# One nine-slot ring for K, V and all weights, K^T written in place, and P·V with V as the stationary operand

## The chip, the cores and the metric

One NeuronCore of a Trainium2 chip. The metric is the device time of one execution in microseconds (us). The engines are written as the profile writes them: PE is TensorE (PEld its weight loads), DVE VectorE, ACT ScalarE, POOL GpSimd, SP SyncE, which here issues the loads; PSUM is the memory that PE writes its results to. Each experiment ran beside the kernel before on the same chip. Ratios are the mean time of one kernel's fast runs over the mean of the other's in the same rounds, so they are not quite the ratios of the medians that I quote. A profile's span is some 2 us shorter than the measured time of the same execution (before: 434.1 against 435.88).

## The reference, cut to what matters

A decode step: one query token, 32 query heads over 4 KV heads, 65,536 cached positions of 128 dimensions, and beside it a gated MLP on the same x.

```python
q = (x @ wq).reshape(1, 1, 32, 128)             # x: 1x1024, wq: 1024x4096
scores = einsum('bhqd,bhkd->bhqk', q, k) * 128 ** -0.5   # k: 4 x 65536 x 128, each for 8 heads
o = einsum('bhqk,bhkd->bhqd', softmax(scores), v)
a = o.reshape(1, 1, 4096) @ wo
z = gelu(x @ w_in);  b = (z1 * (w_sp * layernorm(z2) + b_sp)) @ w_out
out = g * a + (1 - g) * b                       # g = sigmoid(sum(x * gate_w))
```

All of it is bf16. 162.0 MB are read once: K and V 134.2, wq and wo 8.4 each, w_in 7.3, w_out 3.7. There is one query, so every loaded byte is used once.

## The kernel before

K and V come in chunks of 2.1 MB (8192 positions of one KV head), in the order K0 K1 V0 K2 V1 K3 V2 V3, eight chunks each. A chunk of K is turned by TensorE in groups of eight 128x128 tiles. DVE or ACT evicts a turned group from one of three PSUM banks into a small ring, and the scores are taken from there two groups later.

```python
CFG = dict(NSLOT=5, CHUNK_ROWS=8192, RING=5, TBANKS=3, LAG=2, EVPAT="DDA", NALLD=3)
KV  = A("kvarena", [128, NSLOT, CR], BF16)      # five slots for K and V
RNG = A("ktring", [128, R, GPB * 128], BF16)    # K^T, five groups
W   = A("warena", [128, NW, 8192], BF16)        # four slots for the weights
...
# load of a K or V chunk (SyncE, in order): waits until PE has begun the chunk after the one to be replaced
W_.wait("pe_cons", pos - NSLOT + 1)
eng.dma_start(dst, src).then_inc(sb(it["dmasem"]), 16)
...
# one group of K: eight transposes, then the scores of the group two back
eng.matmul(tb[:, j*128:(j+1)*128], kvv[:, t, :], ident_bf[:, :], start=True, stop=True, is_transpose=True)   # L531
eng.tensor_copy(RNG[:, G % R, :], tb[:, :])             # L585, two of three groups (ACT: L587)
eng.matmul(bank[:, t*REP:(t+1)*REP], RNG[:, G % R, j*128:(j+1)*128], qT_bf[...], start=True, stop=True)      # L550
# per chunk: row maximum and copy of the 128x512 scores (DVE)
eng.tensor_reduce(cmax[:, n, :], bank..., AX.X, ALU.max); eng.tensor_copy(scT[:, n, :], bank[:, :])
...
# P.V: p is stationary (8 columns), V moves (128 columns)                                                       L617
eng.matmul(PO[0:REP, 0:DH], pv[:, t, :], vv[:, t, :], start=(c == 0 and t == 0), stop=(...))
# afterwards o (8x128) is scaled, split into hi and lo (two bf16 parts that add up to it), turned by two matmuls, and multiplied by all of wo
```

Exp runs on ACT over a whole KV head at a time: exp of head g while K or V of others are worked on. V(g) waits for it.

## Time and profile before

| | before |
|---|---|
| time, median | 438.09 us (435.88 to 440.12, 4 runs); 438.47 in 16 runs |
| span of the profiled run | 434.1 us |
| busy PE / DVE / ACT | 341 / 190 / 141 us |
| loads | 162.0 MB, 373 GB/s over the span, 425 GB/s at the plateau |
| last load landed | about 412 to 415 us, then 20 us of PE and DVE work |

No engine is busy all the time. The one thing that is nearly always busy is the stream of loads, and the lines that show this are in the prediction. A line of the slices gives 40 equal parts of the span; a line of the windows gives, for 4 us, the busy time and count of each engine, the clock that the throttle granted to TensorE (1.00 is full), the mean share of the 16 DMA engines, and GB/s.

### The profile page before, as it was taken

What the parts mean: (1) busy time and instruction counts of PE and PEld (TensorE: products, weight loads), DVE (VectorE), ACT (ScalarE), POOL (GpSimd) and SP (SyncE); (2) the same over time, 40 slices, a digit from 0 to 9 for tenths busy, and PEclk for the clock granted to TensorE, in tenths of its full rate; (3) what the DMA queues carried; (4) which work ended last, traced back from release to release, by engine and by line L of the source; (5) the groups of instructions that cost most, each with busy time, mean ns of one, the idle gap of its engine ahead of it and who ended that gap; (6) DMA issues with size and microseconds to landing.
All of it is one profiled execution on the core that took longest, in us unless ns stands there. A gap on an engine that the chain in (4) does not pass through costs nothing.

```text
span 434.1 us, 14443 instructions
## 1 busy us (share of the span) xinstructions
PE 341.1 (79%) x6810; PEld 324.6 (75%) x6810; DVE 190.4 (44%) x357; ACT 141.0 (32%) x131; POOL 0.9 (0%) x8
## 2 busy tenths in 40 slices
PE   0059767879888697989798869668889877999994
PEld 0059666868888597988768769568888777988892
DVE  1006644878978600029848730005988720001304
ACT  1003312429944296010124469200034379000000
POOL 0000000000000000000000000000000000000000
PEclk9999988998999889969899979899999989899999
DMA  7998999999999699989999999999999999999900
GB/s 271 427 430 340 426 421 429 427 423 429 417 341 350 226 355 429 430 325 367 415 360 350 402 404 405 416 430 426 426 424 424 421 346 408 425 430 420 408 12 0
DMA packets 17474, 162.94 MB, mean 375 GB/s; under 512 B 1285, under 2 KB 1285, under 8 KB 8198
## 3 DMA queue, kind: packets, MB, share of 16 engines
q1 hardware_dynamic: 17414, 162.02, 91.5%
q8 instruction: 53, 0.87, 0.8%
q14 instruction: 7, 0.06, 0.0%
HBM read 162.01 MB, written 0.00 MB: 373 GB/s over the span
## 4 chain that ended last, share of the span: by engine, by line
PE 46%; DMA 18%; ACT 18%; DVE 15%; issue 2%; SPq 1%; DVEq 0%; ACTq 0%
ACT scT L720 17%; PE ps_tb L531 16%; PE ps_o L617 14%; DMA kvarena<-in_A_k_cache_dram 13%; PE ps_sc L550 8%; DMA warena<-in_A_wq_dram 5%; DVE ktring L585 4%; DVE cmax L637 4%; DVE scT L639 3%; PE ps_m L970 3%; PE ps_m L490 2%; PE ps_m L789 1%; PE ps_m L887 1%; ACT ktring L587 1%; DVE a_sb L986 0%
## 5 line engine op out<-in xcount | busy, mean ns | idle before, releaser
L531 PE MATMUL ps_tb<-ident_bf,kvarena 128*128 128x128 bf16 x2048 | 160.8, 224 | 11.3 <-DMA kvarena<-in_A_k_cache_dram 10.6
L585 DVE COPY ktring<-ps_tb 128x1024 bf16<-128x1024 bf16 x195 | 126.4, 686 | 35.5 <-PE ps_tb L531 35.3
L617 PE MATMUL ps_o<-kvarena,scT 128*8 128x128 bf16 x2048 | 129.0, 230 | 5.9 <-DMA kvarena<-in_A_v_cache_dram 5.4
L617 PEld LDWEIGHTS ps_o<-kvarena,scT 128*8 128x8 bf16 x2048 | 126.6, 92 | 6.7 <-DMA kvarena<-in_A_v_cache_dram 6.0
L531 PEld LDWEIGHTS ps_tb<-ident_bf,kvarena 128*128 128x128 bf16 x2048 | 121.3, 99 | 12.7 <-DMA kvarena<-in_A_k_cache_dram 11.2
L587 ACT ACTIVATE ktring<-ps_tb 128x1024 bf16<-128x1024 bf16 x61 | 62.7, 1028 | 172.5 <-PE ps_tb L531 172.5
L550 PE MATMUL ps_sc<-qT_bf,ktring 128*128 128x8 bf16 x2048 | 89.1, 167 | 22.1 <-DVE ktring L585 20.5
L550 PEld LDWEIGHTS ps_sc<-qT_bf,ktring 128*128 128x128 bf16 x2048 | 76.7, 97 | 27.9 <-DVE ktring L585 25.7
L720 ACT ACTIVATE scT<-scT,nbias 128x512 bf16<-128x512 bf16 x32 | 74.3, 2737 | 14.5 <-DVE nbias L708 14.5
L637 DVE TENSOR_REDUCE cmax<-ps_sc 128x8 f32<-128x512 f32 x32 | 22.1, 691 | 14.0 <-PE ps_sc L550 11.6
L727 DVE CAST rs_hi<-rowsum 128x8 bf16<-128x8 f32 x4 | 0.7, 170 | 55.8 <-ACT scT L720 55.8
L490 PE MATMUL ps_m<-xgT_bf,warena 128*128 128x1 bf16 x256 | 7.1, 165 | 22.1 <-DMA warena<-in_A_wq_dram 20.5
L760 DVE TENSOR_SCALAR o_sb<-ps_o,rcp 8x128 f32<-8x128 f32 x4 | 1.4, 338 | 52.5 <-PE ps_o L617 52.5
L490 PEld LDWEIGHTS ps_m<-xgT_bf,warena 128*128 128x128 bf16 x256 | 7.0, 104 | 22.3 <-issue 22.3
L639 DVE CAST scT<-ps_sc 128x512 bf16<-128x512 f32 x32 | 21.8, 681 | 0.0
L720 ACT ACTIVATION_READ_ACCUMULATOR scT<-scT,nbias 128x1 f32 x32 | 15.9, 497 | 0.0
L970 PE MATMUL ps_m<-warena,oT_bf 128*1 128x256 bf16 x128 | 12.9, 272 | 1.0 <-DVE oT_bf L953 1.0
L498 DVE CAST qT_bf<-ps_m 128x32 bf16<-128x32 f32 x1 | 0.2, 192 | 28.6 <-PE ps_m L490 28.6
L970 PEld LDWEIGHTS ps_m<-warena,oT_bf 128*1 128x1 bf16 x128 | 9.1, 83 | 3.9 <-DVE oT_bf L953 1.4
L986 DVE TENSOR_TENSOR a_sb<-a_sb,ps_m 1x512 f32<-1x512 f32 x6 | 4.1, 685 | 10.0 <-PE ps_m L970 9.9
L798 DVE COPY zT<-ps_m 128x28 f32<-128x28 f32 x1 | 0.2, 188 | 17.7 <-PE ps_m L789 17.7
L738 PE MATMUL ps_m<-ident_bf,rs_hi 128*8 128x128 bf16 x4 | 0.9, 219 | 8.6 <-DVE rs_lo L730 8.6
(86 smaller groups left out, 52.3 us busy)
## 6 DMA issues: line engine op xcount, KB each, us to landing
kvarena<-in_A_k_cache_dram SPq DMA_DIRECT2D x32, 2048.0 KB, 19.0
kvarena<-in_A_v_cache_dram SPq DMA_DIRECT2D x32, 2048.0 KB, 11.9
warena<-in_A_wq_dram SPq DMA_DIRECT2D x4, 2048.0 KB, 14.4
warena<-in_A_wo_dram SPq DMA_DIRECT2D x4, 2048.0 KB, 18.7
warena<-in_B_w_in_dram SPq DMA_DIRECT2D x4, 1792.0 KB, 19.9
warena<-in_B_w_out_dram SPq DMA_DIRECT2D x2, 1792.0 KB, 16.4
xg_raw<-in_A_x_dram SPq DMA_DIRECT2D x1, 2.0 KB
gw_raw<-in_gate_w_dram SPq DMA_DIRECT2D x1, 2.0 KB
```

The source lines that it names most:

```text
L490: mm_ = eng.matmul(PM0[:, QC + h:QC + h + 1], wv[:, t % 2, h * 128:(h + 1) * 128], xgT_bf[:, t:t + 1], start=(t == 0), stop=(t == KT - 1))
L531: mm_ = eng.matmul(tb[:, j * 128:(j + 1) * 128], kvv[:, t, :], ident_bf[:, :], start=True, stop=True, is_transpose=True)
L550: mm_ = eng.matmul(bank[:, t * REP:(t + 1) * REP], RNG[:, G % R, j * 128:(j + 1) * 128], qT_bf[:, g * REP:(g + 1) * REP], start=True, stop ...
L585: eng.tensor_copy(dst, tb[:, :]).then_inc(sb("ev_dve"), 1)
L587: eng.activation(dst, tb[:, :], ACT.Copy).then_inc(sb("ev_act"), 1)
L617: mm_ = eng.matmul(PO[0:REP, 0:DH], pv[:, t, :], vv[:, t, :], start=(c == 0 and t == 0), stop=(c == CPG - 1 and t == T - 1))
L637: eng.tensor_reduce(cmax[:, n, :], bank[:, :].rearrange("p (t h) -> p h t", h=REP), AX.X, ALU.max)
L639: eng.tensor_copy(scT[:, n, :], bank[:, :]).then_inc(sb("dve_evac"), 1)
L720: eng.activation(ap_in, ap_in, ACT.Exp, bias=nbias[:, gh:gh + 1], scale=SCALE, accum_out=rowsum[:, gh:gh + 1]).then_inc(sb("act_exp"), 1)
L789: mm_ = eng.matmul(PM0[:, ZPC + ft:ZPC + ft + 1], wv[:, t % 2, ft * 128:(ft + 1) * 128], xgT_bf[:, t:t + 1], start=(t == 0), stop=(t == KT ...
L887: mm_ = eng.matmul(PM1[row:row + 1, 0:512], hT_bf[:, u:u + 1], wv[:, u % 7, q * 512:(q + 1) * 512], start=(u == 0), stop=(u == NFH - 1), t ...
L970: mm_ = eng.matmul(PM1[row:row + 1, c0:c0 + 256], oT_bf[:, gh:gh + 1], wv[:, gh % 8, q * 256:(q + 1) * 256], start=(k == 0), stop=(k == RE ...
```

## The change

Intent: no buffer of its own for any kind of data. One ring of nine slots takes K, V and every weight in the order of use, so that the loads run further ahead of PE. K^T is written back over K in the same slot, which replaces the K^T ring. P·V is turned round, so that V is the stationary operand and eight columns of p move; o then comes out as 128x8 and needs no transposition. Weights are used one slot at a time, with partial sums added on DVE. The diff, cut to its core (the large part that only moves code and adds partial sums is left out, lines are shortened, and the comments are mine):

```diff
-    NSLOT=5,  RING=5,  LAG=2,  NALLD=3,
+    NSLOT=9,  NALLD=5,  RS_OFF=6.5,  MAXT_OFF=0.40,  Z_OFF=6,
-    RNG = A("ktring", [128, R, GPB * 128], BF16)
-    W = A("warena", [128, NW, 8192], BF16)
...
+    seq_list = [("W", "wq", i_) for i_ in range(4)] + list(raw)     # raw: K0 K1 V0 K2 V1 K3 V2 V3
+    # w_in goes between the chunks of V0, w_out between those of K2, wo 0..2 into K2, K3 and V3, wo 3 at the end
...
-            if pos - NSLOT + 1 >= 1:
-                W_.wait("pe_cons", pos - NSLOT + 1)
+            if pos >= NSLOT:
+                occ = SEQ[pos - NSLOT]          # K: its scores are done; V and W: its last matmul is done
+                W_.wait(occ["rel"][0], occ["rel"][1])
...
-            dst = RNG[:, G % R, :]
+            dst = KV[:, it["slot"], b * GPB * 128:(b + 1) * GPB * 128]
...  # all eight groups of a chunk are turned first, then the scores of the chunk before
-                    mm_ = eng.matmul(PO[0:REP, 0:DH], pv[:, t, :], vv[:, t, :],
+                    mm_ = eng.matmul(PO[:, g * REP:(g + 1) * REP], vv[:, t, :], pv[:, t, :],
...
-            eng.tensor_scalar(o_sb[0:8, g*DH:(g+1)*DH], PO[0:REP, 0:DH], rcp8[0:8, g:g+1], None, op0=ALU.mult)
+            eng.tensor_tensor(oT_bf[:, g*REP:(g+1)*REP], PO[:, g*REP:(g+1)*REP], rcpb[:, g*REP:(g+1)*REP], ALU.mult)
```

## The prediction

> **What bounds the kernel now.** I read the page's forty slices first, then the time windows of 4 us, then the chain of work that ended last, then the timeline of single stretches, and last the waits of the DMA queue.
>
> The slices:
>
> ```profile
> PE   0059767879888697989798869668889877999994
> DVE  1006644878978600029848730005988720001304
> DMA  7998999999999699989999999999999999999900
> GB/s 271 427 430 340 426 421 429 427 423 429 417 341 350 226 355 429 430 325 367 415 360 350 402 404 405 416 430 426 426 424 424 421 346 408 425 430 420 408 12 0
> HBM read 162.01 MB, written 0.00 MB: 373 GB/s over the span
> ```
>
> A slice is 10.85 us. The load stream runs at a plateau of some 425 GB/s, has holes (slices 4, 12 to 15, 18 to 22, 33), and is over two slices before the kernel is. So the kernel is bound by its one stream of 162.01 MB, plus what that stream loses. At 425.5 GB/s the bytes take 380.7 us. The transfer records of the trace show that rows of 2 KB (w_out, wo; 12 MB) move at some 385 GB/s, which adds 2 us: 383 us. By 8 us the stream has moved 1.72 MB, so it starts, in effect, at 4.0. Hence the span: 4.0 start + 383 stream + 25 holes + 22 tail = 434.
>
> The windows show one hole and the tail (columns: window, busy time of PE, PEld, DVE, ACT, POOL, granted clock, DMA share, GB/s):
>
> ```profile
> 144.00:148.00 4.00, 3.11 (x78) 2.88 (x75) 2.63 (x5) 1.02 (x1) 0.00 (x0) 1.00 0.76 317
> 148.00:152.00 4.00, 1.90 (x17) 1.71 (x18) 1.98 (x8) 1.21 (x1) 0.00 (x0) 0.59 0.24 57
> ...
> 408.00:412.00 4.00, 4.00 (x67) 3.60 (x65) 1.37 (x2) 0.00 (x0) 0.00 (x0) 1.00 0.94 393
> 412.00:416.00 4.00, 4.00 (x75) 4.00 (x73) 0.00 (x0) 0.00 (x0) 0.00 (x0) 1.00 0.11 45
> 416.00:420.00 4.00, 4.00 (x76) 4.00 (x73) 0.00 (x0) 0.00 (x0) 0.00 (x0) 1.00 0.00 0
> 420.00:424.00 4.00, 4.00 (x76) 4.00 (x73) 0.00 (x0) 0.00 (x0) 0.00 (x0) 1.00 0.02 4
> ```
>
> After 412 everything has landed and PE works off a backlog of V chunks at 76 matmuls per 4 us, 53 ns each, 3.4 us per chunk of 64. Adding the shortfall of each window against 425: 2.0 us lost at 32 to 36 (the queue waits in order for w_in behind q), 10.9 at 120 to 160, 3.6 at 188 to 204, 4.1 at 224 to 244, 1.2 at 260 to 276, 2.6 at 348 to 364: about 25.
>
> The chain shows why holes come during K: one K chunk is one row maximum (cmax), and these are 6.2 us apart, while 2.097 MB arrive in 4.93 us.
>
> ```profile
> 304.39 0.69 DVE cmax L637
> ...
> 310.61 0.69 DVE cmax L637
> ...
> 316.82 0.69 DVE cmax L637
> ```
>
> PE lags 1.3 us per K chunk. Five slots fill, and the queue waits:
>
> ```profile
> SPq L512 <- PE ps_tb L531: 186.8, 31, 11.2
> SPq L512 <- PE ps_o L617: 141.8, 27, 10.8
> ```
>
> These sums are mostly harmless (a full ring waits for each slot while four other loads run); only where GB/s falls do they cost.
>
> **What the Trainium skill says.** "DMA: Bandwidth & Descriptors", section Where 436 GB/s comes from, gives 435.2 GB/s as the ceiling of the 16 ports; the trace agrees, its full windows being 422 to 430. "TensorE: Matmul & The Clock Gate", section Weight-path perf modes, says that 128 bf16 weight columns load by the fast path; section Back-to-back issue gap says that pairs of weight load and matmul sustain some 81 ns at N=128. The trace is faster: 53 ns for a V matmul, and 27 ns for a 128x128 weight load with one moving column (q projection, below). Section The HAM clock gate says an idle window halves the clock; the trace agrees (0.59 in the window at 148, after PE idled).
>
> ```profile
> 24.79 5.93 PE ps_m L490 x217
> ```
>
> **The change, part by part.**
>
> *PV turned round.* V becomes the stationary 128x128 operand and eight columns of p move. Today: 64 x 53 = 3.4 us. Afterwards it has the shape of the score matmuls, of which eight start within 0.20 us in the timeline (25 ns each), and of the q projection (5.93/217 = 27 ns): 64 x 27 = 1.75 us per chunk. PE saves 1.65 us on each of 32 chunks, 53 us of work. It is off the path where PE waits for V data, but it lets PE recover 4.93 - 1.75 = 3.2 us of lag per V chunk instead of 1.5, and it removes the backlog at the end. The transposition of o also goes (four times o_hi, o_lo, two matmuls and a copy), some 1.2 us of it in the tail.
>
> *K^T in place, nine slots for everything.* The K^T ring and the four weight buffers become four more slots. A K slot is now held until its scores are done, one chunk later.
>
> *Transposes first, scores of the previous chunk afterwards.* PE's work per K chunk: 64 transposes at 56 ns = 3.6, 64 scores at 26 ns = 1.65: 5.25 us. I walked through one chunk by hand. Maximum and cast take DVE 1.3 us after the scores; PE fills the three banks meanwhile (1.35 us); then each transposed group waits for an eviction. With DVE alone (0.61 us per eviction, 8 in 4.88 us in the timeline) the last group is out at 5.0 and the scores at 6.65 us; with every third eviction on ACT I get 5.8 to 6.3, mean 6.1. So a K chunk takes as long as before (6.2); this part gains nothing itself.
>
> *Does the ring hold the lag?* Worst are the 16 K chunks in a row at the start: five of them by DVE alone (5 x 1.7) and eleven mixed (11 x 1.2) give 8.5 + 13 = 21.5 us, 4.4 chunks. When PE starts chunk n, slots up to n-2 are free, so loads up to n+7 are issued: the stream runs dry only when it is 7 chunks, 34 us, ahead. Next the eight V0 chunks: PE catches up in about 12 us, then stands in front of the sum of exp(1) (16 rows of 18.5 us of ACT plus the maximum chain, less those 12: about 10 us, two chunks). Later K runs start with no lag, gain 10 us by themselves and some 6 from the gelu and layernorm chain, and have 34. So I expect no hole that is worth more than 1 to 3 us.
>
> *Weights in the stream.* In the order of use, as ordinary slots; the partial sums of q, z and b add small vector instructions (0.19 us each for q and z, 0.68 for b), beside other work. The 2 us hole at 32 goes.
>
> *The tail.* Last in the stream is wo3, 2 MB after the last V chunk. V7 is done 1.75 us after it lands, long before wo3. After wo3: 32 matmuls of 256 columns, 3.2 us at full clock (timeline: x32 in 3.22) or some 6.8 at half (PE is busy only 35% by then; 256 columns at half of the 2.4 GHz that the same TensorE page gives is 213 ns each, an estimate), then unchanged 5.2 us from the first a_sb addition at 428.9 to the end at 434.1. Tail: 0.3 + 5 + 5.2 = 10.5 instead of 22.
>
> Sum: 4.0 + 383 + 2 + 10.5 = 399.5 of span; holes -23, tail -11.5. The profiled run was 1.8 us above its span and the median 4 above it: 3 more. But 383 contains my 2 us for narrow rows, some of which the plateau already holds, so I take 401 for the time.
>
> **Rivals.**
> 1. *The ring still fills in the first sixteen K chunks.* If a K chunk takes 7.5 us (a slower clock, DVE and ACT out of step), the lag is 16 x 2.6 = 41 us against 34: 7 us of hole, 409. For it: PE, DVE and ACT are chained by three banks. Against: 6.2 is measured with a deeper coupling.
> 2. *V as weights is slow.* The profile's page gives 97 ns mean for a weight load of 128x128; were it not hidden, V would take 6.2 us a chunk, above the 4.93 of its load: 32 x 1.3 = 41 us, and the gain is gone (about 440). Against: the same shape runs at 25 to 27 ns in two places.
> 3. *Head of line.* All loads now wait in one order, weights too; PE standing in front of exp or the layernorm chain could hold a slot that everything waits for: 5 to 10 us, 406 to 411. The windows at 148 and 188 speak for such standing, nine slots against its reaching the stream.
> 4. *Transfer hidden anyway?* No: the stream is the path, its holes cost one for one.
>
> **Range and chances.** Below: stream at 427 and a warm tail, 394. Above: rival 1 or 3 in part, 411. Only rival 2 leads out of "faster" (429.3 is 2%), and two measured rows speak against it: faster 0.95, same 0.04, slower 0.01.
>
> **What would show it.** Right: GB/s above 415 in nearly all slices from the second on, the last byte at 386 to 392, about 10 us of tail, V matmuls 64 within 2 us with PE idle in front of each, cmax still 6 us apart. Wrong: a slice under 380 around 110 to 150 (rival 1 or 3), V chunks above 4.9 us (rival 2), or a plateau below 420 throughout, which no term of mine holds.

## The result, and the profile after

405.4 us median (404.22 to 406.69, 11 runs) against 438.47 (16 runs): ratio 0.9252, 95% interval 0.923 to 0.9275. Predicted: 401.0, range 394 to 411. Faster, inside the range, and 4 us above the forecast.

The slices of the page after, one slice being 10.1 us:

```profile
PE   0339988978897753778999865499989764336334
PEclk9999999999999655569999975579999855558556
DMA  6999999999999999999999999999999999999940
GB/s 259 427 435 429 429 429 429 425 427 430 427 427 422 371 423 426 421 398 430 411 431 430 429 429 427 427 416 430 429 424 432 427 430 425 420 422 429 422 190 0
```

The holes of before have gone, but for slice 14 (371) and slice 18 (398). Slice 14 is under 380, which the prediction had named as a sign of being wrong (its rivals 1 and 3); in size it is 1.2 us of loads. PE is now idle in the V stretches, where it was busiest before. One thing was not in the forecast: the last slice with traffic runs at half rate. The windows show it (same columns as in the prediction):

```profile
136.00:140.00 4.00, 3.01 (x103) 2.74 (x99) 2.96 (x8) 0.00 (x0) 0.00 (x0) 0.50 0.91 333
140.00:144.00 4.00, 3.81 (x136) 3.70 (x136) 0.17 (x1) 3.65 (x3) 0.00 (x0) 0.50 1.04 419
...
380.00:384.00 4.00, 0.94 (x35) 0.94 (x35) 0.00 (x0) 0.00 (x0) 0.00 (x0) 0.50 1.03 415
384.00:388.00 4.00, 1.05 (x40) 0.96 (x37) 0.00 (x0) 0.00 (x0) 0.00 (x0) 0.50 0.60 243
388.00:392.00 4.00, 1.76 (x64) 1.67 (x63) 0.17 (x1) 0.00 (x0) 0.00 (x0) 0.50 0.48 186
```

From 384 on the DMA share is 0.60 and then 0.48: about half of the 16 engines have nothing left, and the others work on for 8 us. The chain of work that ended last (start, us, what):

```profile
94.75 0.69 DVE cmax L628
...
101.33 0.69 DVE cmax L628
...
120.44 0.69 DVE cmax L628
...
126.81 0.69 DVE cmax L628
...
357.54 35.42 DMA kvarena<-in_A_wo_dram
393.09 5.48 PE ps_m L1017 x31
398.59 0.68 DVE a_sb L1033
```

K chunks are 6.58 us apart where DVE evicts alone, and 6.37 here where ACT takes a third (in the stretch from 42.8 to 80.1 six of them take 37.3 us, 6.2 each). So K is no faster than before. The end is the last load, then 5.48 us for the 32 matmuls of wo 3, one of whose records is missing (before: 3.22), then unchanged vector work.

The timeline of PE (start, us, line, operation, count, and the wait before it) shows V chunks late and early in the kernel:

```profile
378.14 1.87 PE L610 MATMUL ps_o<-scT,kvarena 128*128 128x8 bf16 x64 [3.02 <-DMA kvarena<-in_A_v_cache_dram]
...
140.05 3.76 PE L610 MATMUL ps_o<-scT,kvarena 128*128 128x8 bf16 x135
146.27 3.39 PE L610 MATMUL ps_o<-scT,kvarena 128*128 128x8 bf16 x121 [2.46 <-issue]
```

Late in the kernel a V chunk costs 1.87 us and then waits 3 us for the next load. Early, where PE has a backlog to work off, it runs 135 matmuls, stands 2.46 us for something the profile calls issue, and runs 121 more. The list of waits has this at 21.3 us in V alone:

```profile
PEld ps_o L610 <- issue: 21.3, 9, 3.0
```

### The profile page after: what moved, and what is told of

It is laid out like the page before. It is cut to its first block, busy times and chain, and to the rows that moved or that the text cites.

```text
span 403.8 us, 14317 instructions
## 1 busy us (share of the span) xinstructions
PE 284.9 (71%) x6810; PEld 256.9 (64%) x6810; DVE 186.9 (46%) x368; ACT 152.1 (38%) x142; POOL 0.9 (0%) x8
## 4 chain that ended last, share of the span: by engine, by line
PE 44%; DMA 23%; ACT 15%; DVE 12%; issue 4%; SPq 1%; DVEq 0%
PE ps_tb L528 22%; PE ps_sc L546 13%; ACT scT L775 9%; DMA kvarena<-in_A_wo_dram 9%; DMA kvarena<-in_A_v_cache_dram 8%; DMA kvarena<-in_A_k_cache_dram 6%; ACT kvarena L562 6%; DVE kvarena L560 4%; PE ps_m L1017 3%; PE ps_o L610 3%; DVE cmax L628 3%; DVE scT L630 2%; PE ps_m L865 1%; PE ps_m L981 1%; SPq L510 1%
## 5 line engine op out<-in xcount | busy, mean ns | idle before, releaser
L528 PE MATMUL ps_tb<-ident_bf,kvarena 128*128 128x128 bf16 x2048 | 141.1, 225 | 21.8 <-DVE kvarena L560 10.5
L560 DVE COPY kvarena<-ps_tb 128x1024 bf16<-128x1024 bf16 x184 | 118.5, 685 | 20.3 <-PE ps_tb L528 18.2
L562 ACT ACTIVATE kvarena<-ps_tb 128x1024 bf16<-128x1024 bf16 x72 | 73.6, 1023 | 132.4 <-PE ps_tb L528 132.4
L610 PE MATMUL ps_o<-scT,kvarena 128*128 128x8 bf16 x2048 | 58.5, 168 | 38.9 <-DMA kvarena<-in_A_v_cache_dram 20.9
L610 PEld LDWEIGHTS ps_o<-scT,kvarena 128*128 128x128 bf16 x2048 | 56.5, 104 | 40.4 <-issue 21.3
L546 PE MATMUL ps_sc<-qT_bf,kvarena 128*128 128x8 bf16 x2048 | 55.7, 166 | 1.6 <-issue 1.6
L546 PEld LDWEIGHTS ps_sc<-qT_bf,kvarena 128*128 128x128 bf16 x2048 | 54.5, 96 | 1.7 <-issue 1.7
L1017 PE MATMUL ps_m<-kvarena,oT_bf 128*1 128x256 bf16 x128 | 16.7, 323 | 6.4 <-DMA kvarena<-in_A_wo_dram 6.4
L646 PE MATMUL ps_m<-xgT_bf,kvarena 128*128 128x1 bf16 x256 | 7.5, 165 | 15.4 <-DMA kvarena<-in_A_wq_dram 15.4
L646 PEld LDWEIGHTS ps_m<-xgT_bf,kvarena 128*128 128x128 bf16 x256 | 7.1, 104 | 15.7 <-DMA kvarena<-in_A_wq_dram 15.7
L865 PE MATMUL ps_m<-xgT_bf,kvarena 128*128 128x1 bf16 x224 | 7.0, 165 | 7.9 <-issue 7.6
L865 PEld LDWEIGHTS ps_m<-xgT_bf,kvarena 128*128 128x128 bf16 x224 | 6.5, 104 | 8.2 <-issue 7.8
```

Source lines behind the costliest of these rows:

```text
L528: mm_ = eng.matmul(tb[:, j * 128:(j + 1) * 128], kvv[:, t, :], ident_bf[:, :], start=True, stop=True, is_transpose=True)
L546: mm_ = eng.matmul(bank[:, t * REP:(t + 1) * REP], ktg[:, t * 128:(t + 1) * 128], qT_bf[:, g * REP:(g + 1) * REP], start=True, stop=True)
L560: eng.tensor_copy(dst, tb[:, :]).then_inc(sb("ev_dve"), 1)
L562: eng.activation(dst, tb[:, :], ACT.Copy).then_inc(sb("ev_act"), 1)
L610: mm_ = eng.matmul(PO[:, g * REP:(g + 1) * REP], vv[:, t, :], pv[:, t, :], start=(c == 0 and t == 0), stop=(c == CPG - 1 and t == T - 1))
L646: mm_ = eng.matmul(PM0[:, QC + h:QC + h + 1], wv[:, tt, h * 128:(h + 1) * 128], xgT_bf[:, t:t + 1], start=(tt == 0), stop=(tt == 1))
```

## The experiments

My theory: the kernel is bound by its stream of loads; the nine slots carry PE's lag through the sixteen K chunks at the start, and that is the greater part of the gain; the turned P·V is mostly off the path once the ring is there, and pays at the end. The rivals: the turned P·V is the main gain; or the order of the loads, not their reach, is what counts. A second question came from the result: why the end of the stream is slow.

### Ring length: seven slots, five slots, ten slots

```diff
-    NSLOT=9,
+    NSLOT=7,      # a_ns7;  5 in a_ns5;  10 in a_ns10
```

> The changed kernel with seven slots in place of nine, nothing else. Theory (the ring's length carries the PE lag of the first sixteen K chunks): PE's lag at the end of K1 reads about 28 us in the trace (first chunk taken at 30.1, last scores done at 137, 16 loads take 79 us), nine slots leave 34 us and lose about 1 us at 132 to 140. Two slots fewer leave 24.6 us, so some 9 to 10 us more are lost there, little elsewhere: 413 to 416 us. Rival (the turned PV alone does it, the ring had room to spare): 404 to 407.

> The changed kernel with five slots, the number that K and V had before, for K, V and weights together. Theory (ring length): PE can be ahead by three loads, 15 us, against a lag of 28 us in K0 and K1 and 10 to 16 us in the later K stretches: seven slots cost 7.5 us, two more of 4.9 us each make some 17, and the later K stretches add 3 to 8: 425 to 432. If what counts were the order of the loads and the place of K^T rather than the length: 412 to 418.

> The changed kernel with ten slots. What the ring still loses at nine is the dip at 132 to 140 (390 and 333 GB/s, 1.2 us) and one at 168 to 176 (0.8 us). Theory: the first goes, the second may: 404 to 405. Rival (the stream's end is set by engines that also fetch the program, a longer ring only lets the others run further ahead): the last load lands within 1 us of 393.0, its spread over the engines is 8 us or more, time 404.5 to 405.5.

Measured: 412.95 us with seven (ratio 0.9442), 427.05 with five (0.9759), 404.73 with ten (0.9223, interval 0.9189 to 0.9257; nine gave 0.9252 and, in a later control, 0.9241). Forecasts were 413 to 416, 425 to 432 and 404 to 405. The slices of seven, then of five:

```profile
GB/s 259 428 431 431 426 427 431 427 427 412 358 318 335 311 426 423 428 418 416 411 438 424 427 429 429 427 417 429 427 427 429 429 427 427 419 427 429 421 173 0
```

```profile
GB/s 266 428 436 426 434 420 358 349 259 299 319 363 242 407 424 427 430 418 417 360 413 432 423 430 426 429 429 417 428 335 430 417 423 427 430 417 430 432 290 0
```

With seven the new hole lies at slices 10 to 14, which is where K0 and K1 end; with five it begins at slice 7, and the later K stretches get holes too (slices 20 and 30). The rest of the slices agree closely. So the reach of the ring is what removed the holes; the rival of the order of the loads (412 to 418 with five slots) is out. Five slots in the new kernel are worth 11 us against before, which is no more than the turned P·V alone gives in the old kernel (b_pvnew, below, within the noise); nine are worth 33, and a tenth closes the last dip (at 136 to 140 the rate is 420 in place of 333):

```profile
136.00:140.00 4.00, 3.03 (x105) 2.75 (x102) 3.04 (x9) 0.00 (x0) 0.00 (x0) 0.50 1.01 420
```

That is the line of the windows of the run with ten. Its gain in time is about the noise, and 404.73 lies in both forecasts for ten slots. The rival's other sign came true: the spread of the last load over the engines is 9.4 us (8.2 with nine), and this load lands at 391.9 in place of 393.0. What the spread is, is told further down.

### P·V turned back in the kernel after, and turned round alone in the kernel before

a_pvold is the kernel after with P·V as before; o is scaled as 8x128, split and turned by two matmuls again:

```diff
-                    mm_ = eng.matmul(PO[:, g * REP:(g + 1) * REP], vv[:, t, :], pv[:, t, :],
+                    mm_ = eng.matmul(PO[0:REP, 0:DH], pv[:, t, :], vv[:, t, :],
```

> The changed kernel with PV turned back: p stationary, V moving 128 columns, o rescaled as 8 rows and transposed in two matmuls as before. Theory (PV is off the path once nine slots stand before it): V chunks take 3.4 us against 4.93 of a load, the lag after K1 is worked off more slowly, yet stays under 34 us, so GB/s stays up and only the tail grows, by a chunk's rest of 1.7 us and 1.2 us of o transposition: 406 to 410. Rival (the turned PV is the main gain): above 418, with new holes in the K2 and K3 stretches.

Measured 408.28 us (ratio 0.9339), as the theory had it. GB/s stays up, although PE is at its limit throughout:

```profile
PE   0339998979897999889998988988999989979993
GB/s 260 429 431 433 427 431 425 425 432 425 427 430 419 378 419 430 401 416 433 420 430 422 430 429 432 425 414 433 426 427 429 425 433 427 416 428 429 345 69 0
```

The cost is at the end: the loads have landed at 392.8, but PE comes to wo 3 at 399.85, from where it needs 3.22 us. Given the ring, turning P·V is worth about 3 us (ratios 0.9339 and 0.9252).

b_pvnew is the kernel before with P·V turned alone (five slots, K^T ring and weight buffers stay):

```diff
-                mm_ = eng.matmul(PO[0:REP, 0:DH], pv[:, t, :], vv[:, t, :],
+                mm_ = eng.matmul(PO[:, g * REP:(g + 1) * REP], vv[:, t, :], pv[:, t, :],
```

> The kernel before with PV turned round alone: V stationary, eight columns moving, o rescaled as 128x8; five slots, K ring and separate weight buffers stay. Theory: the backlog of 12 us at the end goes and the holes after V stretches shrink by some 2 to 4 us, the holes at 32 and 120 to 160 stay: 420 to 426. If the ring were the only gain: 433 or more. If the turned PV were the whole gain: below 412.

Measured 428.58 us (ratio 0.9801, interval 0.9743 to 0.9859): 9 us, not the 12 to 18 that I expected. In the profiled runs 2.6 us of it are the stream (last landing at 412.2 in place of 414.8), as much as I had forecast for the holes, and 6.7 are the tail (12.6 us in place of 19.3), where I had forecast 12. P·V still ran for 9.4 us after the last landing before, and for 1.9 now; but the 32 matmuls of wo take 4.95 us in place of 3.22, with the clock at 0.50 from 404.6 to 418.2. Most of the holes remain:

```profile
GB/s 269 427 431 349 424 421 428 420 429 426 424 387 298 329 281 432 412 387 381 409 413 327 398 405 403 407 427 427 426 421 430 423 312 387 434 425 426 426 262 0
```

The waits between 150 and 176 say what became of the faster V0. In b_pvnew PE stands before the sum over exp(1):

```profile
PE ps_m L740 <- DVE rs_lo L732: 10.0, 1, 10.0
```

In the kernel before, in the same stretch, it is a quarter of that:

```profile
PE ps_m L738 <- DVE rs_lo L730: 2.4, 1, 2.4
```

What V gains there is given back in the wait for ACT, whose 16 rows of exp hold DVE for 18.6 us either way. That five slots cannot use this time for loads, and nine can, is my reading; no run tests it by itself.

### What a V matmul costs: every one issued twice

```diff
+                    if not (c == 0 and t == 0):
+                        eng.matmul(PO[:, 64:64 + REP], vv[:, t, :], pv[:, t, :], start=False, stop=False)
                     mm_ = eng.matmul(PO[:, g * REP:(g + 1) * REP], vv[:, t, :], pv[:, t, :],
```

> The changed kernel with every PV matmul issued twice (the first into unused columns, the result is not read): V chunks take 3.4 us of PE, 4096 instructions more. Two theories of the end of the stream. Instruction fetch: in the changed kernel's trace the 16 engines finish the last load 8.2 us apart, in two groups of eight, and 53 packets of 16 KB of program travel on the same engines; with 16 packets more the slow group comes about 1 to 2 us later and the spread is 9.5 to 10.5. PV off the path: otherwise the same. The clock stays at full in V, so the last 32 matmuls take 3.2 in place of 5.5 us. Together 404 to 407. Rival (PE time in V still counts): 412 or more. Rival (spread has nothing to do with the program): spread stays at 8.2, time 403 to 404.

Measured 461.38 us (ratio 1.0553): 56 us slower than the kernel after. My number was far off, and so was my picture of what a V matmul costs. By its number the rival, PE time, would have won (412 or more). But PE time can't be the reason: 128 matmuls at 27 ns are 3.4 us, about what a chunk takes in a_pvold, and that ran in 408. The spread of the last load was 2.0 us, which neither forecast had: this stream has holes again, and in every run with large holes late in the stream the last spread is small (3.3 before, 2.4 in b_pvnew). That the engines meet again in a hole is inferred. So this run says nothing about the end of the stream. What differs is the number of instructions: 128 matmuls with their weight loads are 256 instructions a chunk, against 128. The waits of this run:

```profile
PE ps_o L611 <- issue: 34.8, 15, 2.9
PEld ps_o L611 <- issue: 32.5, 16, 3.4
PEld ps_o L612 <- issue: 27.0, 13, 3.0
```

and the windows at the end, before and after the last load has landed (at 428):

```profile
424.00:428.00 4.00, 1.33 (x51) 1.26 (x48) 0.00 (x0) 0.00 (x0) 0.00 (x0) 0.50 0.58 217
...
436.00:440.00 4.00, 4.00 (x162) 4.00 (x159) 0.00 (x0) 0.00 (x0) 0.00 (x0) 0.82 0.02 4
440.00:444.00 4.00, 4.00 (x156) 4.00 (x154) 0.00 (x0) 0.00 (x0) 0.00 (x0) 0.50 0.01 4
```

The same code that stands still for 2.4 us after every 3.4 us while loads run goes without a gap when they don't: 154 to 162 matmuls touch each 4 us from 436 to 448, even at half clock. The Trainium skill, "Runtime: NRT & Kernel Launch", section Instruction fetch mechanics, says that an engine's instructions come in blocks of 16 KiB (256 instructions) over a DMA queue of its own, and that crossing from one to the next is mostly hidden. Whether it is hidden here, the trace can say. The profile counts these packets as the queue of kind instruction:

```profile
q8 instruction: 69, 1.13, 0.9%
```

Read from the trace's transfer records, each is 16 KB. Their number follows PE's instructions: 53, 69 and 37 packets in the kernel after, here, and in a_half10 below, whose PE records (matmuls and weight loads) are 13,620, 17,708 and 9,524. And they release the waits: each of the 12 waits of PE for issue of over 0.8 us in the kernel after ends 2.2 to 2.5 us after one of these packets started, and so do 27 of the 29 in this run.

How often they come: in the kernel after two of them never start less than 5.95 us apart. In this run the distance falls to 3.5 us once the loads have ended, which is the pace of PE itself (128 x 27 ns). It also falls below 5.6 us in other runs, and the records show where: in twelve traces (all but a_lo8, whose last load is in pieces) 25 of 625 distances are under 5.6 us, and in each of the 25 fewer than two loads, on average, were issued and not yet landed; the 538 with two or more are all at least 5.64 us. So while two or more loads are under way, PE gets 256 instructions per 6 us: 128 pairs of weight load and matmul. A V chunk of 64 such pairs costs at least 3.0 us of the fetch, however short its matmuls; one of 128 pairs costs 6.0, more than the 4.93 us of its load. That they came no faster with two or more loads under way is measured; why is not.

### The end of the stream: ten slots with half of the score and P·V matmuls

A load's semaphore is raised once by each of the 16 engines, and the trace records when. First to last engine, for four loads of the kernel after (us):

```
load landing at   9.8:  spread 0.8
load landing at 119.7:  spread 3.4
load landing at 238.7:  spread 5.7
load landing at 393.0:  spread 8.2   (eight engines by 386.5, none until 391.2, eight from there to 393.0)
```

The engines drift apart, at the end in two groups of eight. A program packet takes 0.93 us of an engine. Of the 47 data packets of 16 KB that took over 0.9 us in this trace (the others take 0.61), 45 overlap a program packet in time. Theory: the program rides on the load engines and delays eight of them; since a load is usable when its last engine is done, that lengthens the stream. Test: fewer instructions, same loads. The result is wrong on purpose (the record's check of results passed it all the same, so "correct" says little about the attention part).

```diff
-    NSLOT=9,
+    NSLOT=10,
+        eng.memset(PS[0][:, :], 0.0); eng.memset(PS[1][:, :], 0.0)
         for j, t in enumerate(grp_tiles(G)):
+            if j % 2 == 0: continue                   # scores: odd tiles only
...
-                for t in range(T):
+                for t in range(1, T, 2):              # P.V: odd tiles only
```

> Ten slots, and every second score matmul and every second PV matmul left out (wrong result on purpose): 4096 PE instructions fewer, the same loads. Theory (program fetches ride on the load engines and delay eight of them): some 16 of the 53 program packets go, the spread of the last landing falls from 9.4 us to 6.0 to 7.2, the last landing from 391.9 to about 389.5 to 390.5, and PE's waits for issue in V (a 16 KB packet of 256 instructions comes no oftener than every 6 us while loads run) vanish, since a V chunk now has 64 instructions: time 402 to 403. Rival (the spread is the engines' own, from the data): spread 9 us or more, landing within 0.5 us of 391.9, time 404.5.

Measured 401.27 us (ratio 0.915; ten slots with the whole program: 0.9223). The page counts 37 program packets in place of 53:

```profile
q8 instruction: 37, 0.61, 0.5%
```

The last load lands at 389.3 in place of 391.9, its spread is 7.6 in place of 9.4 (a little above my 6.0 to 7.2), and 34 data packets are slow in place of 52, 32 of them beside a program packet. The time is below the forecast of 402 to 403. PE no longer waits for issue in P·V (its one such wait in the trace is 0.2 us, elsewhere), as the theory of the fetch had it. The rival, a spread of the engines' own, had nothing moving (9 us or more, landing within 0.5 us of 391.9). a_best below, with ten slots and the whole program on the same chip as this run, repeats the comparison: 391.7 and 9.5.

There is one more rival: half the matmuls could free slots earlier, so that the ring waits less. The transfer records rule it out: in both runs 16 or more packets are in flight from 10 to 380 us, in all but 0.1 us of it. So it is shown that instructions lengthen the stream: 16 packets, 2.6 us. Scaled to all 53 (an estimate from these two numbers, and only if the effect is linear), 8.6 us of the stream are program, and without it the last landing would be near 383. It is not shown that the whole spread comes from the program: with 30% of the packets gone it fell by 19%. That the packets lie on just the eight late engines is inferred, since the records do not name the engine, and it can't be all: the first engine is done 0.8 us earlier too (381.7 against 382.5).

### The last load on eight engines

```diff
-                eng.dma_start(dst, src).then_inc(sb(it["dmasem"]), 16)
+                for p in range(0, 128, 8):            # wo 3 only
+                    eng.dma_start(dst[p:p + 8], src[p:p + 8]).then_inc(sb(it["dmasem"]), 16)
```

> The changed kernel with the last load, wo3, cut into 16 pieces of 8 partitions, which by the Trainium skill (DMA: Bandwidth & Descriptors, Why a DMA increments its semaphore by 16) go to the lowest eight of the 16 engines alone. In the trace the engines finish the load before at 379.7 to 381.4 (eight of them) and 386.1 to 387.9 (the other eight). 2 MB on eight engines take 10.5 us at the rate of 2 KB rows. If the lowest eight are the early ones: last landing 390.5, time 402.5 to 403.5. If they are the late ones, or mixed: landing 398, time 410 to 411.

Measured 417.08 us (ratio 0.9505), outside both forecasts, so the time settles nothing about the engines: SyncE took 37 us to issue the 16 pieces, one of which took it 14 us, so the last piece landed at 404.1 for that reason alone. The transfer records say more. From 380.5 to 385, while eight engines were still busy with the 16 KB packets of the last V chunk, six packets of 2 KB (wo 3) were in flight on average. So of the eight engines that took the pieces about six are early ones and two late: the groups are mixed with respect to this choice. Which engines the late ones are stays open.

### A warm TensorE at the end

```diff
+                if g == HKV - 1 and c >= 4:
+                    W_.wait("dve_evac", NKC)
+                    for _k in range(10 if c < CPG - 1 else 12):
+                        eng.matmul(PS[0][:, 0:512], ident_bf[:, :], scT[:, 0, :], start=True, stop=True)
```

> The changed kernel with 10 to 12 matmuls of 512 columns, whose results are not read, after each of the last four V chunks, so that PE stays busy. Theory (the tail's 32 matmuls run at half clock since PE idles): they take 3.2 in place of 5.46 us, granted clock 1.0 from 370 on, time 403 to 403.5. Rival (the clock isn't what slows them): 405 to 406.

Measured 403.93 us (ratio 0.9213, interval 0.9177 to 0.925, which overlaps those of the kernel after, so the gain is not clear of the noise in time). The chain shows that both the theory and my dose were half right:

```profile
389.59 4.22 PE ps_sc L620 x11
393.81 3.17 PE ps_m L1021 x32
```

The 32 matmuls take 3.17 us in place of 5.48, at a clock of 1.00 (0.50 from 392 to 396 in the kernel after), so the clock was the reason. But the clock did not stay at 1.00 from 370 on: it fell to 0.50 at 390.2, in the midst of the twelve unused matmuls after the last V chunk, which start 0.21 us apart before that and 0.43 after. They took 4.2 us and ended 1.0 us after the load had landed (392.8).

### A control, and the pieces together

after_again is the kernel after, unaltered.

> The changed kernel unaltered, as a yardstick on the same chip for the runs beside it: 404 to 407, ratio near 0.925.

Measured 404.64 us, ratio 0.9241 (0.9207 to 0.9274).

a_best has ten slots, seven warming matmuls after the last V chunk in place of twelve, and less vector work after the last matmul:

```diff
+            if g == HKV - 2:                          # while wo 3 is still loading
+                eng.tensor_scalar(b_sb, b_sb, omg, None, op0=ALU.mult)
+                eng.scalar_tensor_tensor(a_sb, a_sb, g_sb, b_sb, op0=ALU.mult, op1=ALU.add)
-                    ins_ = eng.tensor_tensor(dst, dst, src, ALU.add)          # last group
+                    eng.scalar_tensor_tensor(out_bf[0:1, half], src, g_sb, dst, op0=ALU.mult, op1=ALU.add)
-        eng.tensor_scalar(b_sb, b_sb, omg, ...); eng.scalar_tensor_tensor(out_bf, a_sb, g_sb, b_sb, ...)
```

> Ten slots, warming matmuls in the last four V chunks (7 after the last one, so that they end before wo3 lands), and the tail's vector work cut: b times (1 - g) plus g times the first three parts of a is formed while wo3 is still loading, so that after the last matmul two scalar_tensor_tensor of 512 elements (1.4 us) take the place of two additions, a scaling and a 1024-element combination (3.5 us). Ten slots gave -0.7, warm -1.5 with 1 us lost to the dummies' length, the vector part -2.1: 400 to 401.5. If the single gains don't add: 402 to 403.

Measured 400.07 us (399.99 to 400.19, correct), ratio 0.9127 (0.9097 to 0.9157), beside 0.9241 of the control on the same chip. It beats both kernels. Its chain ends:

```profile
391.87 3.23 PE ps_m L1021 x32
395.13 0.74 DVE out_bf L1042
```

The 32 matmuls of wo 3 start 0.2 us after the last landing (391.7) and run at full clock, and two short vector instructions follow. Which of the three pieces gave how much was not taken apart.

## Why the prediction was right, point by point

- **The bound is the stream, and its holes cost one for one.** Right. Holes of 25 us became about 2 to 3 (ring-length runs: slots taken away come back as a hole at the place that was named).
- **The ring holds the lag of sixteen K chunks.** Right, with a smaller margin than forecast. K chunks took 6.2 and 6.58 us against my 6.1 and 6.65. But one took 8.1, when the maximum chain of exp(0) came between (cmax at 86.66 and 94.75), and the last scores ended at 137.0, after a first chunk begun at 30.1: 107 us for 79 us of loads, a lag of 28 us where I had summed 21.5. Against the 34 us of nine slots that should have fitted, and it did not quite: the dip at 132 to 140, which ten slots close, costs 1.2 us; why the sum missed it was not traced. It is slice 14 with its 371 GB/s, so the prediction's own sign for rivals 1 and 3 appeared, at 1.2 us of the 7 and the 5 to 10 that these had.
- **PE recovers 3.2 us of lag per V chunk (4.93 - 1.75).** This step failed. A chunk alone costs 1.87 us, near my 1.75, but sustained work is held to 256 instructions per 6 us while loads run, so two V chunks take 6 us, and PE recovers 1.9 us per chunk and not 3.2. I had read 27 ns from bursts of at most 217 matmuls, the longest of which was followed by "issue" in the chain of before: the sign was there. It cost little here, because in V0 PE had to stand before exp(1) anyway, and the loads are slower than 3.0 us a chunk; at most it shares in the dip at 168 to 176 (0.8 us), where two waits for issue fall (2.4 and 2.6 us). That the total came out inside the range in spite of this step is luck: the change had slack where the step was wrong. In a_pv2 it costs 56 us.
- **Rival 2, V as weights is slow.** It did not happen, but it was nearer than I thought: with twice the instructions it does happen, for a reason that I had not listed.
- **The stream takes 383 us, the last byte comes at 389 with holes.** The last landing was at 393.0, just outside the 386 to 392 of the forecast; this term was 4 us too small, and that is nearly the whole of the miss (403.8 of span against 399.5). The plateau of 425 is the mean of 16 engines of which eight run ahead; the end is set by the other eight, which seem to carry the program too (inferred, see above). The prediction had no term for either.
- **The tail.** 10.8 us (393.0 to 403.8) against 10.5. Within it the 32 matmuls took 5.48 us, between my 3.2 and 6.8; a_warm shows that the clock was the reason.
- **Two readings in the working.** 53 ns per V matmul of the kernel before comes from counts that include the matmuls at the edges of a window; from start to start they are 55.8 ns apart, so a chunk took 3.6 us. And "full windows 422 to 430" fits the slices: single windows of 4 us read up to 445 (56 to 60), so they are no test of a ceiling of 435. Neither moves the sum by much.
- **What the parts are worth.** The prediction put 23 us on the holes and 11.5 on the tail, and held that the K part gains nothing itself; the runs agree. Alone, the turned P·V gives 9 us in the old kernel; with the ring it gives 3. The two gains overlap; I put this down to the end of the kernel, where a ring that keeps PE close behind the stream leaves less backlog to shorten.

## What to carry to other kernels

Where one stream of loads is the bound, look for the longest run of work that is slower than its loads, sum its lag, and give the ring that much reach: here 1.3 to 1.7 us per chunk over 16 chunks needed nine slots, and each slot short cost 4 to 7 us. Buffers that serve one kind of data each are idle reach; putting them into one ring gave it without new memory. And count instructions as well as their time: where loads filled the DMA engines here, the program came beside them, which held small matmuls to 128 pairs per 6 us and lengthened the stream. A ring that keeps many loads under way does not make this better: the distance was under 5.6 us only with fewer than two of them. A K chunk is 128 pairs too (64 transposes, 64 scores) and takes 6.0 to 6.6 us; made much faster, it would meet the same limit (an inference, not tested).

## What the Trainium skill lacked or had wrong

- "Runtime: NRT & Kernel Launch", Instruction fetch mechanics, calls the fetch of 16 KiB blocks mostly hidden. Here it is not: while two or more loads are under way, two blocks of PE's program never start less than 5.6 us apart (5.95 in the kernel after), and PE stands up to 3.0 us for the next one (21.3 us in V). In a_pv2 with the loads over, blocks for P·V come every 3.5 to 3.8 us and PE does not wait.
- "DMA: Bandwidth & Descriptors", section Queues, rings and completion order, has a runtime row for refills on the same engines that carry the data. No page has what this costs a long stream: the spread of one load's 16 completions grows from 0.8 to 8.2 us, and 16 program packets fewer bring the last landing forward by 2.6 us.
- "TensorE: Matmul & The Clock Gate", The HAM clock gate, ties the half clock to idle windows. In a_pv2 PE was busy for 4.00 of 4 us in each window from 436 to 448 with matmuls of eight columns, and the clock fell from full to 0.50 (0.82, 0.50, 0.50 in the three windows); in the kernel after it is 1.00 in the K stretch from 35.9 to 134.9 and 0.50 in V0. So busy time in the profile is not what the gate sees. Such matmuls lose nothing by it (26 to 27 ns from start to start at 0.50).
- The same page, Back-to-back issue gap, gives 81 ns for sustained pairs at N=128. In the kernel before, pairs at N=128 start 55 to 56 ns apart, both the transposes (128 weight columns) and the V matmuls (8 weight columns).
